# Other SBUF addresses: the values ahead of P, the turned inputs swapped, the pools of mixer and spatial stage in another sequence with empty stretches

## The chip, the cores and the metric

The kernel runs on one core of one Trainium2 chip. The metric is the device time of one execution in microseconds (us); three runs of the kernel before gave 2320.51, 2326.43 and 2330.06 us, so its median is 2326.43 us. Engines are named as in the profile: PE (TensorE matmul), PEld (its weight load), DVE (VectorE), ACT (ScalarE), POOL (GpSimd) and SP (SyncE, which here only issues DMAs, one after the other, in a fixed order).

## The reference, cut to what matters

Two different layers are applied in turn, twice over, to an input x of 2048 rows of 640 numbers:

```
x = x + A(layernorm(x))     # attention, 32 heads of 20, four segments of 512 rows, with a memory
x = x + B(layernorm(x))     # gated MLP with a mixing over the rows
x = x + A(layernorm(x))
x = x + B(layernorm(x))

A:  q, k, v = x @ wq, x @ wk, x @ wv
    for each segment: p = softmax(q k^T * scale + mask);  o = g * memory part + (1 - g) * p v
    return o @ wo
B:  z = gelu(x @ w_in);  z1, z2 = halves of z (864 wide each);  z2 = layernorm(z2)
    g = w_sp @ z2 + b_sp            # w_sp is 2048 x 2048: mixes the rows
    return (z1 * g) @ w_out
```

## The kernel before, in words

Each layer pair runs as three stages, one after the other in the program text. Large products are made from f16 parts: a number is split into a high part and the rest (h and l), and three products h*h, h*l, l*h are summed.

- **Attention** (`phase1a`, class `Attention`). Tiles of 128 rows are normalised (`prep`, L643), split, turned by a DMA transpose into `xt0` or `xt1` (segments take turns), and `value` (L663) multiplies them into `vs0` or `vs1`, first tiles 0 to 3, then the rest while the loop runs. `unit` makes q and k; the loop makes logits twice, exponentials into `P` and `Pb` (L909), their split into PH (L943) and PL (L945), the product with the values (L973). The o tiles go to DRAM (L1005). The projection with wo (`project`, L705) of tiles 0 to 11 fills PE; its rows stand in two buffers `xt` of pool `ae2` and are stored as x1 (L713).
- **Mixer** (`phase1b`). For each of 16 row tiles: layernorm, split (L264, L265), DMA transpose into `th` (L266), 30 matmuls with each half of w_in (L341), gelu, and the second half normalised and kept in SBUF as `zh` and `zl` (L349, L350), the first half stored to DRAM as z1 (L355). For tiles 12 to 15 the projection with wo is done here (L318), from tiles `o` and `xt`. In the first layer pair the first half of w_in is split here into `wi0h` and `wi0l` from five staged pieces `wst` (L115 load, L80 on ACT, L81 on DVE); in the second it is read back already split.
- **Spatial stage** (`phase2`). For each of 16 row tiles of w_sp, `rows(t)` loads 1 MB into `wr` (one buffer, L402), takes the row maxima on DVE (L404), scales and splits into `wn` (two buffers, L414 on ACT, L415 on DVE) and turns it by two DMA transposes into `wt` (two buffers, L416). `spatial(t)` does 96 matmuls `gp` (L427) over all of zh and zl, adds the bias (L430), multiplies with `cz1`, the reloaded z1 (L432), takes maxima (L434), splits (`un`, L440, L441) and turns (`ut`, L443). `tail(t)` does 42 matmuls `cyp` with w_out (L456), adds `cx1`, the reloaded x1 (L459), and stores the result. `spatial(t)` stands in the program ahead of `rows(t + 1)`, that ahead of `tail(t - 1)`.

**What sets the order.** In attention PE's order is written out by hand. Everything else (DVE, ACT, POOL, SP always, PE in the other stages) is ordered when the kernel is built: a planner plays the program through with its own durations, and each engine's next instruction is the ready one of highest priority, where earlier in the program is higher and `high_priority(offset=n)` counts as n instructions earlier. `rows(0)` and the loading of wi0 have the offset 2000, the first steps of the mixer 300; the mixer's whole program is about 1800 instructions long. On the chip each engine then works through its list strictly in that order, and waits at the first instruction whose inputs are not there.

**What addresses have to do with it.** SBUF is a stack: pools of a stage lie one behind the other in the sequence in which they are opened, pools with `side="right"` from the other end. When a stage ends its pools go, and the next stage's pools lie on the same bytes. With `reuse_waits="tile"` a new tile waits for exactly those earlier tiles whose bytes it covers. So a tile's address decides which last uses of the stage before it waits for. These are the places in bytes of a partition, summed from the sizes of the tiles (each rounded up to 32):

```
attention, before                      attention, after
 44064 qk0-4, vs1, mxs                  44064 the same
 65312 P                                65312 vs0
 85792 PL, rs, ab                       75808 PL, rs, ab
 93600 PH, gm                           83616 PH, gm
108960 mr                               98976 mr
109472 vs0                              99488 P
119968 phq, hl, tmp, den, mst, pk      119968 the same
145312 ae2: xt, xh (two each)          145312 xt1
155552 xt0                             155552 xt0
165792 xt1                             165792 ae2: xt, xh (two each)
176032 staging, qk5, Pb                176032 the same, to 193536

mixer, before (zh 44064, zl 71712)     mixer, after (zh, zl the same)
 99360 z1 z1, z2                        99360 z1 z1, z2
109728 x1 x1                           109728 o
114848 th th th                        112288 empty, 7808 bytes
122528 xn, xnhl                        120096 x1 x1
127648 wi0h, wi0l                      125216 th th th
144928 wst wst                         132896 xn, xnhl
151840 xt xt                           138016 wst wst
156960 o, to 159520                    144928 wi0h, wi0l
                                       162208 xt xt, to 167328

spatial stage, before                  spatial stage, after
 99360 u, un, ut                        99360 the same
109984 cz1 cz1, cx1 cx1, xo xo         109984 the same
127136 wuh, wul, bsp                   127136 the same
145120 wr                              145120 empty, 22336 bytes
153312 wn wn                           167456 wr
161504 wt wt, to 177888                175648 wn wn
                                       183840 wt wt, to 200224
```

From the right end, unchanged: `wi1h`, `wi1l` at 212064, `woh`, `wol` at 199264, both until the mixer ends, and in the spatial stage the staging of w_out at 222432.

Of the kernel before, what the change touches and what calls it, by code (L numbers as in the profile page):

```python
# [8 lines left out]
F32 = mybir.dt.float32  # L9
# [272 lines left out]
def phase1b(g, o_d, x, x1_d, z1_d, zh, zl):  # L282
    nc, tc = g.nc, g.tc
    with ExitStack() as ctx:
        pool = lambda n, b, **k: ctx.enter_context(tc.tile_pool(name=n, bufs=b, reuse_waits="tile", **k))
        p2, p1, pe2, pe3, pe1 = pool("b2", 2), pool("b1", 1), pool("be2", 2), pool("be3", 3), pool("be1", 1)
        wp0, sp, px2, px1 = pool("bw0", 1), pool("bs", 2), pool("bx2", 2), pool("bx1", 1)
        pz1, py, pz0 = pool("bz1", 2, space=PSUM), pool("by", 1, space=PSUM), pool("bz0", 1, space=PSUM)
        g.wi[0].tiles(wp0)
        wi0 = g.wi[0].load(sp)  # L290
# [87 lines left out]
def phase2(g, w_sp, b_sp, x1_d, z1_d, zh, zl, out):  # L378
    nc, tc = g.nc, g.tc
    KO = 7  # L380
    with ExitStack() as ctx:
        pool = lambda n, b, **k: ctx.enter_context(tc.tile_pool(name=n, bufs=b, reuse_waits="tile", **k))
        p1, p2, wp = pool("c1", 1), pool("c2", 2), pool("cw", 1)
        pr, ph, pt2, sp = pool("cr", 1), pool("ch", 2), pool("ctr", 2), pool("cs", 2, side="right")
        pg = pool("cg", 2, space=PSUM)
        py = pool("cy", 2, space=PSUM)
# [184 lines left out]
class Attention:  # L571
# [40 lines left out]
    def setup(self, ctx):  # L612
        g, nc, tc = self.g, self.nc, self.tc
        pool = lambda n, b, **k: ctx.enter_context(tc.tile_pool(name=n, bufs=b, reuse_waits="tile", **k))
        sk, p3, self.pl2, self.pl3, self.pr = pool("ak", 1), pool("a3", 1), pool("al2", 2), pool("al3", 3), pool("amr", 1)
        av, self.u4, self.u2, self.u1 = pool("av", 1), pool("au4", 4), pool("au2", 2), pool("au1", 1)
        self.e2, self.e1, ax = pool("ae2", 2), pool("ae1", 1), [pool(f"ax{i}", 1) for i in range(2)]
        self.pl1, self.bg = pool("al1", 1), pool("abg", 2)
        self.pd = pool("apd", 2, space=PSUM)
        self.px = pool("apx", 1, space=PSUM)  # L620
        self.pm = pool("apm", 1, space=PSUM)
        self.pe = pool("ape", 1, space=PSUM)
        self.po = pool("apo", 1, space=PSUM)
        more = pool("aqk", 1)
        self.Pb = pool("aP", 1).tile([128, 2, 1280], F32, name="Pb")
        self.qk = [(sk if i < 5 else more).tile([128, 2, L], F16, name=f"qk{i}") for i in range(self.NQK)]
        self.Pf = p3.tile([128, 2, 2, 1280], F32, name="P")
        self.vs = [p.tile([128, 4, H, 2 * DH + 1], F16, name=f"vs{i}") for i, p in enumerate((av, sk))]
        for t in self.vs:
            nc.gpsimd.memset(t[:, :, :, DH:DH + 1], 1.0)  # L630
        self.xt = [p.tile([128, 2, KD, L], F16, name=f"xt{i}") for i, p in enumerate(ax)]
        self.mxs = [sk.tile([128, 64], F32, name=f"mxs{i}") for i in range(2)]
        self.mst = [self.u1.tile([128, NU, 8, DH + 1], F32, name=f"mst{i}") for i in range(2)]
# [602 lines left out]
```

## Time and profile before

| | |
|---|---|
| median of three runs | 2326.43 us |
| the profiled execution: its own time | 2327.81 us |
| the profiled execution: span from first to last instruction | 2326.0 us |
| PE busy | 2171.9 us (93%) |
| DVE, ACT, POOL busy | 1375.1, 1139.1, 987.1 us |

The page of the profile gives busy times, the span in 40 slices and the costliest groups; the chain of waits is followed back from the last instruction to what released each step. A timeline lists instructions in order with their start and length, and in square brackets how long the engine had been idle and what ended that. A table by windows gives for each stretch its bounds, its length, each engine's busy time with its number of instructions, the granted TensorE clock, and the DMA engines' share and rate. All times in these views count from the start of the span.

### The profile page before, as it was taken

What the parts mean: (1) busy time and instruction counts of PE and PEld (TensorE: products, weight loads), DVE (VectorE), ACT (ScalarE), POOL (GpSimd) and SP (SyncE); (2) the same over time, 40 slices, a digit from 0 to 9 for tenths busy, and PEclk for the clock granted to TensorE, in tenths of its full rate; (3) what the DMA queues carried; (4) which work ended last, traced back from release to release, by engine and by line L of the source; (5) the groups of instructions that cost most, each with busy time, mean ns of one, the idle gap of its engine ahead of it and who ended that gap; (6) DMA issues with size and microseconds to landing.
All of it is one profiled execution on the core that took longest, in us unless ns stands there. A gap on an engine that the chain in (4) does not pass through costs nothing.

```text
span 2326.0 us, 52573 instructions
## 1 busy us (share of the span) xinstructions
PE 2171.9 (93%) x21706; PEld 1306.4 (56%) x21706; DVE 1375.1 (59%) x2577; ACT 1139.1 (49%) x1344; POOL 987.1 (42%) x976
## 2 busy tenths in 40 slices
PE   5888899999899999999998989999999999999998
PEld 3455555666555545555554556566665554555554
DVE  7688879677544545443427786877765453544331
ACT  3587788887522322121126987888863221112110
POOL 2387889999511000000014988899991100000000
PEclk9999999999999999999999999999999999999999
DMA  5565665345644587665534465443564347666561
GB/s 168 153 159 149 165 176 130 88 124 145 167 109 100 145 232 170 164 166 150 134 90 114 110 161 128 124 106 109 134 163 108 94 116 216 163 164 159 156 148 44
DMA packets 504912, 325.59 MB, mean 140 GB/s; under 512 B 410688, under 2 KB 445632, under 8 KB 499552
## 3 DMA queue, kind: packets, MB, share of 16 engines
q1 hardware_dynamic: 504672, 322.23, 53.9%
q8 instruction: 170, 2.79, 0.5%
q14 instruction: 70, 0.57, 0.1%
HBM read 148.46 MB, written 85.61 MB: 101 GB/s over the span
## 4 chain that ended last, share of the span: by engine, by line
PE 61%; DVE 12%; DMA 9%; POOL 7%; ACT 6%; issue 4%; SPq 2%; DVEq 0%; ACTq 0%; POOLq 0%
PE gp L427 19%; PE zp L341 13%; PE cyp L456 7%; POOL PL L945 5%; PE qps L732 3%; PE pv L973 3%; DMA wr<-in_B_w_sp_dram 3%; PE vps L673 2%; PE kps L732 2%; PE mp L871 2%; DVE mxs L934 2%; PE yps L705 2%; ACT P L909 2%; ACT PH L943 2%; PE es L871 1%
## 5 line engine op out<-in xcount | busy, mean ns | idle before, releaser
L945 POOL TENSOR_TENSOR PL<-P,PH 128x640 f16<-128x640 f32 x380 | 536.2, 1436 | 53.1 <-PE pv L973 43.6
L427 PE MATMUL gp<-zh,wt 128*128 128x432 f16 x2048 | 463.3, 346 | 4.5 <-DMA wt<-wn 4.5
L427 PEld LDWEIGHTS <-wt 128*128 128x128 f16 x3072 | 300.4, 98 | 262.6 <-DMA wt<-wn 5.3
L934 DVE TENSOR_REDUCE mxs<-mp 128x2 f32<-128x1024 f32 (+2 forms) x384 | 320.3, 862 | 136.4 <-PE mp L862 134.9
L909 ACT ACTIVATE P<-es,sc 128x1024 f32<-128x1024 f32 (+1 forms) x256 | 271.6, 1061 | 95.4 <-PE es L862 87.4
L442 POOL MEMSET un<- 128x64 f16 x32 | 5.0, 155 | 692.6 <-DMA ut<-un 648.0
L341 PEld LDWEIGHTS <-th 128*128 128x128 f16 x1920 | 187.5, 98 | 166.4 <-issue 3.5
L427 PE MATMUL gp<-zl,wt 128*128 128x432 f16 x1024 | 270.6, 346 | 0.0
L943 ACT CAST PH<-P 128x1280 f16<-128x1280 f32 x192 | 239.7, 1248 | 1.6
L252 POOL TENSOR_TENSOR lnrs<-lnve,mhalf 128x1 f32<-128x1 f32 x96 | 59.8, 631 | 423.8 <-DVE lnve L251 410.2
L430 ACT ACTIVATE u<-gp,bsp,un 128x864 f32<-128x864 f32 x32 | 34.2, 1068 | 363.3 <-PE gp L427 360.4
L404 DVE TENSOR_REDUCE am<-wr 128x1 f32<-128x2048 f32 x32 | 73.1, 2286 | 221.9 <-DMA wr<-in_B_w_sp_dram 221.9
L456 PE MATMUL cyp<-wuh,ut 128*128 128x320 f16 (+1 forms) x896 | 170.1, 308 | 14.1 <-DMA ut<-un 14.0
L945 POOL TENSOR_TENSOR PL<-Pb,PH 128x640 f16<-128x640 f32 x124 | 178.6, 1467 | 8.1 <-PE pv L973 8.0
L673 PE MATMUL vps<-wvh,xt 128*128 128x320 f16 x640 | 156.9, 314 | 26.7 <-DVE relu L764 19.2
L456 PEld LDWEIGHTS <-ut 128*128 128x128 f16 (+1 forms) x1344 | 134.6, 101 | 75.3 <-DMA ut<-un 16.8
L414 ACT ACTIVATE wn<-wr,ivw 128x1024 f16<-128x1024 f32 x64 | 72.0, 1144 | 204.5 <-DVE ivw L409 129.6
L871 PEld LDWEIGHTS <-qk 64*128 64x128 f16 (+1 forms) x2048 | 78.5, 94 | 159.5 <-issue 140.1
L973 PE MATMUL pv<-vs,PL 128*128 128x41 f16 x2560 | 157.0, 181 | 7.5 <-POOL PL L945 5.2
L973 PE MATMUL pv<-vs,PH 128*128 128x41 f16 x2560 | 159.4, 182 | 2.8 <-DVE ab L989 2.8
L341 PE MATMUL zp<-wi0h,th 128*128 128x432 f16 x640 | 148.5, 346 | 1.1 <-ACT z L354 1.1
L341 PE MATMUL zp<-wi1h,th 128*128 128x432 f16 x640 | 148.0, 346 | 1.3 <-DMA th<-xnhl 1.3
(189 smaller groups left out, 4347.4 us busy)
## 6 DMA issues: line engine op xcount, KB each, us to landing
wr<-in_B_w_sp_dram SPq DMA_DIRECT2D x32, 1024.0 KB
qk<-st SPq DMA_DIRECT2D x256, 120.0 KB
z<-z SPq DMA_DIRECT2D x32, 432.0 KB
cz<-z SPq DMA_DIRECT2D x32, 432.0 KB
xt<-in_A_x_dram SPq DMA_DIRECT2D x32, 320.0 KB
st<-qhl SPq DMA_DIRECT2D x40, 256.0 KB
st<-khl SPq DMA_DIRECT2D x40, 256.0 KB
x<-x SPq DMA_DIRECT2D x32, 320.0 KB
```

Source lines behind the costliest of these rows:

```text
L341: nc.tensor.matmul(zp[:, n, :FHH], a[:, k, :], b[:, k, c:c + FHH], start=(k == 0 and j == 0), stop=(k == KD - 1 and j == 2))
L404: nc.vector.tensor_reduce(am, wr, AX.X, ALU.max, apply_absolute_value=True)
L427: nc.tensor.matmul(gp[:, n, :FHH], wt[:, k // 8, a, k % 8, :], b[:, k, n * FHH:(n + 1) * FHH], start=(k == 0 and j == 0), stop=(k == NT - ...
L456: nc.tensor.matmul(yp[:, n, :320], a[:kn[k], k, :], b[:kn[k], k, n * 320:(n + 1) * 320], start=(k == 0 and j == 0), stop=(k == KO - 1 and ...
L673: nc.tensor.matmul(ps, a[:, k, c], b[:, k, n * 320:(n + 1) * 320], start=(i == 0), stop=(i == 14))
L732: nc.tensor.matmul(ps, a[:, k, c], b[:, k, :], start=(i == 0), stop=(i == 14))
L871: nc.tensor.matmul(out[:, h, o:o + w], a[r, ac], b[r, bc], start=o == 0, stop=False, skip_group_check=True)
L909: self.lead.append(nc.scalar.activation(P, E, AF.Exp, scale=g.esc))
L934: e = nc.vector.tensor_reduce(mx[:, :, n, j], mp[:, :, o:o + w], AX.X, ALU.max)
L943: nc.scalar.copy(PH, P[:, h])
L945: (nc.gpsimd if h == 0 or n < self.N - self.TAIL else nc.vector).tensor_tensor(PL[:, c], P[:, h, c], PH[:, c], ALU.subtract)
L973: nc.tensor.matmul(pv[:, i, h, :], x[:, c:c + 128], v[:, j, h0 + h, :], start=(j == 0 and x is PH), stop=(j == i and x is PL), skip_group_ ...
```

## The change

Only pools and their sequence change; every instruction's operation and shape stays. In attention the pool of `vs0` moves ahead of the pool of `P`, `xt1` comes ahead of `xt0`, both ahead of `ae2`, and the pool `ae1`, which held nothing, is gone. In the mixer `o` moves to the front, an empty stretch follows, the staging comes ahead of wi0, and `xt` goes last. In the spatial stage an empty stretch goes in ahead of `wr`. The tiles named gap are never written or read.

```
 phase1b
-        p2, p1, pe2, pe3, pe1 = pool("b2", 2), pool("b1", 1), pool("be2", 2), pool("be3", 3), pool("be1", 1)
-        wp0, sp, px2, px1 = pool("bw0", 1), pool("bs", 2), pool("bx2", 2), pool("bx1", 1)
+        p2, p1, px1, gap = pool("b2", 2), pool("b1", 1), pool("bx1", 1), pool("bgap", 1)
+        pe2, pe3, pe1 = pool("be2", 2), pool("be3", 3), pool("be1", 1)
+        sp, wp0, px2 = pool("bs", 2), pool("bw0", 1), pool("bx2", 2)
+        gap.tile([128, 1945], F32, tag="gap", name="gap")
 phase2
-        p1, p2, wp = pool("c1", 1), pool("c2", 2), pool("cw", 1)
+        p1, p2, wp, gap = pool("c1", 1), pool("c2", 2), pool("cw", 1), pool("cgap", 1)
+        gap.tile([128, 5580], F32, tag="gap", name="gap")
 Attention.setup
-        sk, p3, self.pl2, self.pl3, self.pr = pool("ak", 1), pool("a3", 1), pool("al2", 2), pool("al3", 3), pool("amr", 1)
-        av, self.u4, self.u2, self.u1 = pool("av", 1), pool("au4", 4), pool("au2", 2), pool("au1", 1)
-        self.e2, self.e1, ax = pool("ae2", 2), pool("ae1", 1), [pool(f"ax{i}", 1) for i in range(2)]
+        sk, av, self.pl2, self.pl3, self.pr, p3 = pool("ak", 1), pool("av", 1), pool("al2", 2), pool("al3", 3), pool("amr", 1), pool("a3", 1)
+        self.u4, self.u2, self.u1 = pool("au4", 4), pool("au2", 2), pool("au1", 1)
+        ax1, ax0, self.e2 = pool("ax1", 1), pool("ax0", 1), pool("ae2", 2)
+        ax = ax0, ax1
```

## The prediction

> **What bounds the kernel now.** I read the page first, then PE's idle time by windows, then the chain of waits, and last the timeline at each gap. From the page, the span and PE:
>
> ```profile
> span 2326.0 us, 52573 instructions
> PE 2171.9 (93%) x21706; PEld 1306.4 (56%) x21706; DVE 1375.1 (59%) x2577; ACT 1139.1 (49%) x1344; POOL 987.1 (42%) x976
> ```
>
> PE is busy 93%. An edit that only moves addresses changes no instruction, so it can win only where PE waits for something that an address decides, and an address decides only what a stage's first tiles wait for. So I cut the span at the joints of the stages. Columns: stretch, its length, then busy time of PE, PEld, DVE, ACT, POOL with counts, granted clock, DMA share and rate.
>
> ```profile
> 618.00:809.00 191.00, 186.70 (x1052) 102.57 (x1051) 101.13 (x197) 60.21 (x69) 19.73 (x30) 1.00 0.48 130
> 809.00:860.00 51.00, 45.52 (x242) 24.56 (x241) 23.88 (x40) 14.29 (x16) 0.30 (x2) 0.90 0.84 228
> 860.00:1173.00 313.00, 313.00 (x1857) 181.34 (x1855) 131.73 (x234) 54.45 (x52) 7.13 (x20) 1.00 0.64 157
> 1173.00:1206.00 33.00, 29.64 (x205) 20.41 (x204) 11.58 (x26) 7.09 (x12) 6.92 (x7) 0.95 0.40 97
> 1750.00:1936.00 186.00, 186.00 (x1052) 102.72 (x1051) 96.31 (x192) 56.79 (x65) 18.81 (x30) 1.00 0.43 109
> 1936.00:2060.00 124.00, 116.69 (x662) 65.65 (x661) 52.90 (x93) 23.64 (x23) 0.91 (x6) 0.97 0.77 198
> ```
>
> Inside the mixer and the spatial stage PE never rests (313.00 of 313.00, 186.00 of 186.00). It rests at three joints: start of the spatial stage in the first pair (809 to 860) and in the second (1936 to 2060), and the passage from the first spatial stage to the second attention (1173 to 1206). There the clock is below 1 as well. The gaps one by one, from PE's timeline:
>
> ```profile
> 841.15 0.90 PE L427 MATMUL gp<-zh,wt 128*128 128x432 f16 x2 [2.11 <-DMA wt<-wn]
> 845.42 0.71 PE L456 MATMUL cyp<-wuh,ut 128*128 128x320 f16 x2 [3.37 <-DMA ut<-un]
> 1184.05 0.45 PE L456 MATMUL cyp<-wuh,ut 128*128 128x320 f16 x2 [0.93 <-DMA ut<-un]
> 1192.36 0.30 PE L673 MATMUL vps<-wvh,xt 128*128 128x320 f16 x1 [2.43 <-DVE vs L679]
> 1968.58 0.54 PE L427 MATMUL gp<-zh,wt 128*128 128x432 f16 x2 [2.38 <-DMA wt<-wn]
> 1973.08 0.45 PE L456 MATMUL cyp<-wuh,ut 128*128 128x320 f16 x2 [2.32 <-DMA ut<-un]
> 2045.40 0.45 PE L456 MATMUL cyp<-wuh,ut 128*128 128x320 f16 x2 [2.51 <-DMA ut<-un]
> ```
>
> After such a gap the next matmuls run slowly: windows over L456 alone (length, PE busy, PEld busy, clock, DMA) show the same 42 matmuls in 8.79, 7.56 and 7.55 us at clock 0.68 and 0.79, and in 5.88 us at clock 1.00.
>
> ```profile
> 845.00:855.00 10.00, 8.79 (x42) 5.21 (x42) 0.68 0.72 232
> 1973.00:1981.00 8.00, 7.56 (x42) 4.71 (x42) 0.79 0.44 174
> 2045.00:2053.00 8.00, 7.55 (x42) 4.73 (x42) 0.79 0.86 174
> 1184.00:1190.00 6.00, 5.88 (x42) 4.03 (x42) 1.00 0.41 128
> ```
>
> The Trainium skill, "TensorE: Matmul & The Clock Gate", Part 1, puts the drop to half clock after an idle window of about 3.4 us; taken as a threshold, only the gap of 3.37 us could carry a tail. The trace disagrees: gaps of 2.32 to 2.51 us carry one too. By the threshold the sum below would lose its tails after those gaps, 3.35 + 1.41 us; by the rows they stand, and I take the rows.
>
> **Start of the spatial stage.** The chain of waits shows what is late there (start, length, what), and a full mixer tile and a full gp for measure:
>
> ```profile
> 746.57 10.95 PE zp L341 x60
> 817.10 9.79 DMA wr<-in_B_w_sp_dram
> 877.07 17.52 PE gp L427 x96
> 1922.31 6.18 DMA wr<-in_B_w_sp_dram
> 1945.31 12.13 DMA wr<-in_B_w_sp_dram
> ```
>
> The third w_sp tile, for gp(2), is requested at 817.10 and 1945.31, when the stage has begun. On DVE, the reduce that waits for it stands ahead of the steps for u(0):
>
> ```profile
> 826.91 2.29 DVE L404 TENSOR_REDUCE am<-wr 128x1 f32<-128x2048 f32 x1 [2.29 <-DMA wr<-in_B_w_sp_dram]
> 829.89 1.06 DVE L432 TENSOR_TENSOR u<-u,cz 128x864 f32<-128x864 f32 x1
> 1953.93 1.06 DVE L432 TENSOR_TENSOR u<-u,cz 128x864 f32<-128x864 f32 x1 [17.83 <-DMA cz<-z]
> 833.96 6.82 SPq L416 DMA_TRANSPOSE wt<-wn  x2
> 840.88 2.10 SPq L443 DMA_TRANSPOSE ut<-un  x1
> ```
>
> So wt(2) is turned from 833.96, after PE has almost finished gp(1), and ut(0) only behind it at 840.88; PE waits for both. In the second pair the first wait on DVE is for cz1. Addresses cause this. Before, `wr` at 145120 and `wn` at 153312 cover the mixer's `wst`, `xt` and `o`, and `xt` and `o` serve tiles 12 to 15, the mixer's end. So rows(0) can't begin before that, and as wr is one buffer, rows(1) and rows(2) follow one load each later. After, wr, wn and wt begin at 167456, behind the mixer's last byte (167328). Only attention's tiles lie there, gone since the mixer began; wt's second buffer also touches woh, whose last use is tile 15's projection in the mixer. So rows(0), rows(1) up to its transposes, and wr(2) have the whole mixer for themselves, and wt(2) waits for gp(0) alone. The `cz1` and `cx1` tiles before cover x1 and th of the mixer; after, mostly `o` and the empty stretch, so their loads too can go ahead of the crowd.
>
> If so, both waits go in both pairs. First pair: 2.11 + 3.37 = 5.48 us idle plus 8.79 - 5.88 = 2.91 us of slow pace: 8.4. Second pair: 2.38 + 2.32 + 2.51 = 7.21 idle plus (7.56 - 5.88) + (7.55 - 5.88) = 3.35: 10.6. Together 19.0. What is late next is the ut chain of some later tile, which has one whole gp (17.5 us) of cover; I take nine tenths, **17 us**.
>
> **Spatial stage to second attention.** Before, `vs0` at 109472 covers ut, both cz1 and both cx1; all are in use until the last tail. So the values of tile 0 stand in PSUM until L459 is done:
>
> ```profile
> 1190.32 0.88 DVE L459 SCALAR_TENSOR_TENSOR xo<-cyp,xs,cx 128x640 f32<-128x640 f32 x1
> 1191.24 0.78 ACT L678 ACTIVATE vs<-vps 128x320 f16<-128x320 f32 x2
> ```
>
> ACT starts 0.04 us after it. After, vs0 at 65312 covers zh and zl, free when gp(15) ends, and its memset on POOL (L630) comes forward with it. Then value tile 1 follows tile 0 (the 30 matmuls in the first row below), fills the wait for ut of 0.93 us, and the 2.43 us go. For tiles 2 and 3 to be in time, xt0 must be filled earlier: before it covers wn and wt; after, the empty stretch, so its transposes wait for nothing. The pace:
>
> ```profile
> 1178.00:1184.00 6.00, 4.24 (x30) 2.93 (x30) 1.00 1.12 230
> 1192.00:1199.00 7.00, 6.64 (x37) 4.33 (x38) 0.76 0.54 143
> ```
>
> 37 of these at the first row's pace take 5.23 us, so 1.41 are lost. Sum 0.93 + 2.43 + 1.41 = **4.8 us**.
>
> **Attention to mixer, first pair.** `wst` before covers `pk` and the `xt` and `xh` buffers of ae2, which the last projection and the last o tile use; its loads go out behind that store, and PE waits for the split once:
>
> ```profile
> 612.45 0.95 SPq L115 DMA_DIRECT2D wst<-in_B_w_in_dram  x2
> PE zp L341 <- DVE wi0l L81: 1.9, 1, 1.9
> ```
>
> After, wst covers mst and pk, whose last reads come with the last segment's memory, steps ahead of attention's end. **1.9 us** gained. But the five splits, by their priority, now run inside attention:
>
> ```profile
> L81 DVE SCALAR_TENSOR_TENSOR wi0l<-wst,iv,wi0h x5: 1108/1112/1118, 619.6 to 633.3; 128x864 f16<-128x864 f32 x5
> L81 DVE SCALAR_TENSOR_TENSOR wol<-wst,iv,woh x5: 876/1179/1706, 250.8 to 265.9; 128x640 f16<-128x640 f32 x5
> ```
>
> The same operation takes up to 1706 ns inside attention and 876 at best. The Trainium skill, "SBUF — State Buffer", Who interferes with whom, has a rule against this move: a DVE instruction with two SBUF inputs and a GpSimd one that reads SBUF block each other for the whole instruction. The slowest wol row agrees. By the rule at its worst all five take what that row shows, and the gain would be smaller by 10.8 - 1.9 = 8.9 us. My cost goes by rows: between 0 (hidden, as PE is the busier engine) and 5 x 1.112 x 1706/876 = 10.8 us (all on the path). The nearest row is wol's median, 1179 against 876, a third more: 5 x 1.112 x 0.35 = **1.9 us**, which I take.
>
> **What the early rows cost.** They come at the mixer's start, where before they ran at its end, hidden. Of rows(t) DVE does:
>
> ```profile
> L404 DVE TENSOR_REDUCE am<-wr x32: 2279/2286/2289, 781.8 to 2227.5; 128x1 f32<-128x2048 f32 x32
> L415 DVE SCALAR_TENSOR_TENSOR wn<-wr,ivw,wn x64: 1273/1280/1286, 787.0 to 2241.8; 128x1024 f16<-128x1024 f32 x64
> DVE am L404 <- DMA wr<-in_B_w_sp_dram: 221.9, 31, 11.3
> ```
>
> That is 2.29 + 2 x 1.28 = 4.9 us, and ahead of the reduce DVE stood still 221.9/31 = 7.2 us on average: the planner lists it before the load has landed. What is queued behind it on DVE is the layernorm and split of the next th tile, and PE waits for that. At most 12.1 us per row; a mixer tile takes 10.95 us of PE and 53% of DVE (101.13 of 191), so 5.1 us of DVE are free per tile and at most 7.0 come through. At least 0, as in the second pair before, where the load of 1922.31 and the one ahead of it were taken in between 1750 and 1936 and PE lost nothing. ACT has 60.21 us of work in 191, so its two scalings per row hide. Rows(0) has priority over the whole mixer and meets it where th is not yet ahead; I take **2 us** in each pair, and nothing for rows(1) and rows(2), which come last in priority. SP's list gains nothing, its DMAs only move; it passes th's transposes, in the same 2 us. The mixer's other moves (x1, th, xn over phq, hl, tmp; zl over PL, PH, gm; z2 over P) cover tiles done before the first write; they cost nothing. If gm's last use were late, zl would wait, and PE not, as zl is needed only by gp. In the first attention the moves wait for nothing, as no stage came ahead.
>
> **Sum.** 17 + 4.8 + 1.9 - 1.9 - 4 = 17.8 us. The profiled execution took 2327.81 us, 1.4 above the median of 2326.43; on the median's basis 2326.43 - 17.8 = **2308.6 us**. Bounds of the terms: with all of 19.0 and no cost 25.7, so 2301; with costs of 10.8 and 2 x 7.0 the 23.7 are eaten and 1.1 more, so 2328.
>
> **Rivals.**
> - *The gain is given back at the mixer's start.* Rows(0) costs its full 7.0 us in both pairs and the splits half of their upper bound, 5: 23.7 - 14 - 5 = 5 us gained, 2322. For it: the 7.2 us that DVE stood before L404. Against: the full stretch of 1750 to 1936, above, with two such loads in it. Chance 0.17.
> - *The planner does not use the freedom.* It still lists the loads late, or wn and wt bind; then the passage to the second attention remains and, say, three tenths of the start: 4.8 + 0.3 x 19 - 2 = 8 us, 2318. For it: rows(1) and rows(2) come last in priority. Against: the load at 1922.31 is rows(1)'s and was issued inside the mixer, ahead of the stage's start at 1936. Chance 0.14.
> - *Slower.* Rows(0), (1) and (2) each hold DVE inside the mixer beyond its 5.1 us of slack per tile and PE waits each time: 3 x 7.0 x 2 = 42, less 23.7, 18 us more, 2345. It decides once the standstill per row passes about 5 us inside the mixer. Against: DMA there is busy 0.43 to 0.48, at the spatial start 0.84, so loads should land sooner than the 7.2. Chance 0.09.
>
> My forecast has the remaining 0.60, with 2297 to 2317 as its own range.
>
> **How the numbers follow.** Half a per cent of the median, 11.6 us, is about what a measurement of this kernel can tell from no change: faster means below 2314.8, slower above 2338.1. Faster: 0.55 of the forecast's 0.60, 0.07 of the second rival, 0.02 of the first: 0.64. Slower: 0.09. Same: 0.27. The range runs from 2294 (planner luck in attention beyond the bounds) to 2326, which takes in the first two rivals and leaves out the slower one and the tails, under 0.2.
>
> **What would show it.** In the changed profile: three wr loads ahead of 809 and of 1936, the first soon after attention's end; no PE gap ended by wt or ut in the spatial stage's first 60 us of either pair; vs0's ACT right after its matmuls, and value tiles in one run at clock 1; L115 for wi0 well ahead of 612. Wrong would be: new PE gaps ended by th between 615 and 660 or 1745 and 1790, with DVE standing before L404; a longer first attention; or gaps at the spatial stage's start that stay.

## The result, and the profile after

The changed kernel takes 2315.67 us (median of nine runs, 2304.89 to 2320.03) where the kernel before takes 2327.17 (nine runs beside it, 2320.51 to 2333.34). The recorded ratio is 0.9936, 95% interval 0.9923 to 0.9949: 15 us or 0.64% faster (0.0064 x 2327), 12 to 18 by the interval; the two medians by themselves are 11.5 us apart. Its profiled execution is the slowest of the nine, 2320.03 us, so a second profile was taken (run e8 below, 2311.18 us). Three executions far off all others (5012.18 us of run e10, which was the profiled one, and 2770.27 and 12151.94 us of the kernel before, beside later runs) are left out of the ratios.

The page of the changed kernel, span and engines:

```profile
span 2318.3 us, 52548 instructions
PE 2174.6 (94%) x21706; PEld 1309.5 (56%) x21706; DVE 1377.8 (59%) x2577; ACT 1139.2 (49%) x1344; POOL 991.4 (43%) x976
```

The five engines' counts are those of before; the 25 fewer of the total are instructions that do not count as busy. The table by windows, over the same stretches of work as before, shifted to where they now lie:

```profile
624.50:812.00 187.50, 185.15 (x1045) 101.90 (x1044) 100.33 (x200) 58.03 (x66) 18.38 (x28) 1.00 0.52 127
812.00:863.00 51.00, 50.15 (x287) 27.77 (x285) 25.40 (x41) 14.85 (x16) 0.30 (x2) 1.00 0.87 237
1164.00:1197.00 33.00, 33.00 (x234) 22.77 (x233) 9.01 (x17) 5.25 (x9) 1.39 (x3) 1.00 0.22 55
1753.00:1941.00 188.00, 183.53 (x1036) 100.83 (x1034) 101.12 (x200) 57.35 (x65) 18.37 (x28) 1.00 0.48 117
1941.00:2065.00 124.00, 124.00 (x727) 70.99 (x726) 50.27 (x89) 22.88 (x22) 0.91 (x6) 1.00 0.72 177
```

All three joints are closed. At the spatial starts PE is busy 50.15 of 51 us (before 45.52) and 124.00 of 124 (before 116.69), in the passage 33.00 of 33 (before 29.64), and the granted clock is 1.00 where it was 0.90, 0.95 and 0.97. In return the second mixer, full before (186.00 of 186.00), now has 4.47 us in which PE stands idle. The gaps that are left, from PE's timeline:

```profile
594.86 0.61 PE L875 MATMUL es<-qk 64*128 64x384 f16 x4 [2.59 <-ACT P L913]
645.73 0.54 PE L343 MATMUL zp<-wi1h,th 128*128 128x432 f16 x2 [1.29 <-DMA th<-xnhl]
791.40 0.54 PE L343 MATMUL zp<-wi1h,th 128*128 128x432 f16 x2 [1.06 <-DMA th<-xnhl]
847.54 0.44 PE L459 MATMUL cyp<-wuh,ut 128*128 128x320 f16 x2 [0.85 <-DMA ut<-un]
1759.58 0.54 PE L343 MATMUL zp<-wi1h,th 128*128 128x432 f16 x2 [0.89 <-DMA th<-xnhl]
1773.14 0.54 PE L343 MATMUL zp<-wi1h,th 128*128 128x432 f16 x2 [2.43 <-DMA th<-xnhl]
1918.90 0.54 PE L343 MATMUL zp<-wi1h,th 128*128 128x432 f16 x2 [1.15 <-DMA th<-xnhl]
```

(`zp` is the mixer's product with w_in. Line numbers are those of each kernel's own file; the changed kernel's lie 2 to 4 above those of before.) Of the seven gaps at the joints one of 0.85 us is left. The longest inside attention's end is now 2.59 us, and five gaps in the mixers are ended by th; the second mixer had none before.

The clearest account is the length of each stage from PE's own records: the mixer M from its first zp to its last; S from there to the last gp; the passage P from there to the last matmul of value tile 3 of the next attention; A from the span's start, or from the passage's end, to the first zp. The last column ends with the last cyp. Times in us of one profiled execution each:

| kernel | A1 | M1 | S1 | P | A2 | M2 | S2, tail included |
|---|---|---|---|---|---|---|---|
| before | 607.4 | 201.2 | 364.8 | 33.1 | 533.1 | 196.2 | 386.3 |
| changed | 613.6 | 199.5 | 356.2 | 27.7 | 541.9 | 201.8 | 373.7 |
| changed, second profile (e8) | 613.0 | 199.2 | 356.3 | 27.7 | 536.0 | 200.4 | 372.9 |
| e1 spatial stage alone | 606.4 | 202.1 | 362.8 | 30.9 | 533.2 | 198.7 | 374.2 |
| e2 attention alone | 621.5 | 198.3 | 363.9 | 39.8 | 541.4 | 198.3 | 383.7 |
| e3 mixer alone | 605.4 | 197.6 | 382.8 | 32.7 | 533.3 | 197.0 | 400.8 |
| e7 changed, attention put back | 605.3 | 206.7 | 363.9 | 30.9 | 537.6 | 206.3 | 373.2 |
| e4 changed, wi0 later | 601.4 | 206.1 | 356.6 | 27.7 | 535.7 | 200.1 | 373.9 |
| e5 changed, rows(0) at tile 8 | 612.1 | 199.8 | 356.0 | 27.7 | 533.6 | 198.1 | 373.8 |
| e6 changed, rows(0) at tile 3 | 613.6 | 197.8 | 356.2 | 27.7 | 537.9 | 198.2 | 374.1 |
| e9 as e6, wt clear of woh | 615.3 | 202.2 | 356.6 | 27.7 | 537.1 | 202.3 | 374.6 |
| e12 as e9, rows apart | 617.4 | 200.1 | 356.4 | 27.7 | 533.4 | 198.6 | 374.5 |
| e11 as e1, x of attention later | 612.7 | 202.3 | 356.4 | 32.6 | 533.5 | 198.7 | 373.8 |

S and P repeat within 0.8 us between the two profiles of the changed kernel, M within 1.4; A does not: old and unchanged attention pools alone gave 605 to 613 for A1 and 533 to 538 for A2. So the stages other than attention are read from profiles, and totals from the timed ratios.

How much a wait at the mixer's start costs can't be read at its third tile, because PE fills part of such waits with matmuls of the projection with wo (`yp`) that it would else do later: 30 of them in the first three tiles of the first mixer before, 24 in both mixers of the changed kernel, 14 where nothing waits; 30 take 4.1 us. By the start of tile 12 all kernels have done the same work. Counted from the mixer's first zp to there, in us:

| kernel | first mixer | second mixer |
|---|---|---|
| before | 144.51 | 139.55 |
| changed | 141.01 | 143.22 |
| changed, second profile (e8) | 140.70 | 141.85 |
| e1 | 143.76 | 140.17 |
| e4 | 147.69 | 141.55 |
| e5 | 141.25 | 139.55 |
| e6 | 139.55 | 139.55 |

139.55 us is thus a mixer without waits up to there. In the rest of the mixer, the changed kernel loses 1.3 us in each pair to a gap near the end, and does three gp more (0.5 us) before the last zp; those are taken from S.

### The profile page after: what moved, and what is told of

It is laid out like the page before. It is cut to its first block, busy times and chain, and to the rows that moved or that the text cites. A ratio compares the mean times of both kernels' runs of the same rounds, so it can differ in the third digit from the quotient of the medians.

```text
span 2318.3 us, 52548 instructions
## 1 busy us (share of the span) xinstructions
PE 2174.6 (94%) x21706; PEld 1309.5 (56%) x21706; DVE 1377.8 (59%) x2577; ACT 1139.2 (49%) x1344; POOL 991.4 (43%) x976
## 3 DMA queue, kind: packets, MB, share of 16 engines
q8 instruction: 170, 2.79, 0.5%
## 4 chain that ended last, share of the span: by engine, by line
PE 66%; DVE 9%; DMA 8%; POOL 6%; ACT 6%; issue 3%; SPq 1%; DVEq 0%; ACTq 0%; POOLq 0%
PE gp L430 23%; PE zp L343 13%; PE cyp L459 8%; POOL PL L949 5%; PE pv L977 3%; PE qps L736 3%; PE kps L736 3%; PE vps L677 3%; PE mp L875 3%; DVE mxs L938 2%; PE yps L709 2%; PE es L875 2%; ACT P L913 1%; ACT PH L947 1%; DMA th<-xnhl 1%
## 5 line engine op out<-in xcount | busy, mean ns | idle before, releaser
L949 POOL TENSOR_TENSOR PL<-P,PH 128x640 f16<-128x640 f32 x380 | 538.8, 1444 | 53.2 <-PE pv L977 45.6
L949 POOL TENSOR_TENSOR PL<-Pb,PH 128x640 f16<-128x640 f32 x124 | 178.0, 1462 | 9.2 <-PE pv L977 9.2
L459 PE MATMUL cyp<-wuh,ut 128*128 128x320 f16 (+1 forms) x896 | 165.1, 301 | 5.7 <-DMA ut<-un 5.7
L459 PEld LDWEIGHTS <-ut 128*128 128x128 f16 (+1 forms) x1344 | 132.1, 98 | 61.5 <-DMA ut<-un 6.4
L875 PE MATMUL es<-qk 64*128 64x512 f16 (+3 forms) x1024 | 126.3, 303 | 31.7 <-ACT P L913 27.1
```

Source lines behind the costliest of these rows:

```text
L459: nc.tensor.matmul(yp[:, n, :320], a[:kn[k], k, :], b[:kn[k], k, n * 320:(n + 1) * 320], start=(k == 0 and j == 0), stop=(k == KO - 1 and ...
L875: nc.tensor.matmul(out[:, h, o:o + w], a[r, ac], b[r, bc], start=o == 0, stop=False, skip_group_check=True)
L949: (nc.gpsimd if h == 0 or n < self.N - self.TAIL else nc.vector).tensor_tensor(PL[:, c], P[:, h, c], PH[:, c], ALU.subtract)
```

## The experiments

**Three parts, one at a time (e1, e2, e3).** Of e1 the edit is

```
+        gap.tile([128, 5580], F32, tag="gap", name="gap")    # spatial stage only
```

and e2 and e3 are the kernel before with attention's or the mixer's lines of the diff alone.

> The kernel before, with one line of the change: the empty stretch ahead of wr in the spatial stage; the mixer's and attention's pools stay. Theory (wr's address alone decides the start of the spatial stage, and it also brings the cost at the mixer's start): the spatial start is 8 us shorter in the first pair and 11 in the second, as in the changed kernel; the two waits for wr and th at the mixer's start come with it, about 1 to 5 us in each pair; the passage to the second attention and the end of the first attention stay as before. Together about 12 us below the kernel before. Rival (the moves of cz1, cx1 and the mixer's o are needed too): less than half of that, under 6 us, with gaps left at the spatial start.

e1 took 2320.49 us, ratio 0.9968 (0.9954 to 0.9982): 7.5 us, about two thirds of what the theory gave. Both spatial starts closed as in the changed kernel (up to the 480th gp the first gained 7.6 us, the second 11.4 by its end), so wr's address alone does that; the rival falls. The cost at the mixer's start, expected at 1 to 5 us per pair, is 0.6 in the second pair by tile 12 and none in the first. But S1 as a whole gained 2.0 only. SP's timeline of e1 shows why:

```profile
859.83 0.32 SPq L649 DMA_DIRECT2D xt<-x  x1
1005.68 0.32 SPq L649 DMA_DIRECT2D xt<-x  x1
```

From 859.83 to 1005.68 seven x tiles for the second attention are loaded, normalised and turned, on DVE and SP, between the spatial stage's own steps, and PE waits (3.34 us for ut at 936.21 alone). In e1 attention's `ae2` still lies at 145312, on the new empty stretch, and may be filled at any time. The changed kernel's `ae2` lies on `wr`, so its first such load comes at 1128.46.

> The kernel with the spatial stage's empty stretch alone, and one more edit: the loads of x for the second attention are planned behind the store of tile 12's result. Theory (with the old attention pools ae2 lies on the empty stretch, so seven x tiles were normalised and turned between 860 and 1010, ahead of the spatial stage's own steps on DVE and SP; PE waited 3.3 us at 944 and the stage lost 6.2 us; in the changed kernel ae2 lies on wr's bytes and waits by itself): the loss of 6.2 us between gp 480 and the last gp of the first pair goes to under 1, the rest stays; 4 to 7 us below the kernel with the empty stretch alone. Rival (that loss has another cause, such as cz and cx at their old places): it stays.

> The kernel with the spatial stage's empty stretch alone and x's loads for the second attention planned behind the store of tile 12's result, once more, since the first profile of it fell on an execution of 5012 us. Theory: between gp 480 and the last gp of the first pair nothing is lost against the kernel before (6.2 us were, without the second edit), both spatial starts keep their gain, and the time is 4 to 7 us below that of the empty stretch alone. Rival: the loss stays.

The edit, on top of e1:

```
             s = nc.sync.dma_start(out[t], xo.rearrange("p n c -> p (n c)"))
+            if t == 12:
+                g.late = s
 # in prep, from the second attention on
+            c2.enter_context(self.tc.issue_after(g.late.ins))
             nc.sync.dma_start(xt, self.x[t])
```

e10 took 2316.69 us (median of all five), ratio 0.9940 (0.9916 to 0.9963). e11, the same kernel, took 2310.65 us, ratio 0.9927 (0.9907 to 0.9946): 6.5 and 9.6 us below e1, each against the kernel before (0.0028 and 0.0041 of 2330). In e11's profile the loads come at 1137.29 and later and S1 is 356.4, with nothing lost after the 480th gp. So the loss was the early x tiles. This kernel keeps the old attention and mixer and is about as fast as the whole change.

> The kernel before, with the attention pools of the change alone. Theory (vs0 clear of cz1 and cx1 is what makes the passage shorter): the passage from the first spatial stage to the second attention is 4 to 5.4 us shorter, all gaps at both spatial starts stay as before. wst at 144928 then covers pk and xt1, so the wi0 splits may come forward too; if they do, the first attention ends some 5 us later and the first mixer's start is some 4 us shorter, near zero together. In all 4 to 6 us below the kernel before. Rival (the passage is shorter in the changed kernel because the spatial stage's own tail moved): no change at the passage, 0 in all.

e2 took 2352.24 us, ratio 1.0107 (1.0082 to 1.0131): 25 us slower, both theory and rival wrong. PE's timeline:

```profile
621.52 0.90 PE L341 MATMUL zp<-wi1h,th 128*128 128x432 f16 x2 [7.66 <-DMA th<-xnhl]
1197.70 0.71 PE L456 MATMUL cyp<-wuh,ut 128*128 128x320 f16 x2 [8.25 <-DMA ut<-un]
```

and SP's:

```profile
606.78 0.80 SPq L300 DMA_DIRECT2D x<-x  x2
1170.23 13.87 SPq L649 DMA_DIRECT2D xt<-x  x2
```

P at 99488 to 119968 now lies under the old mixer's z1 and x1, and P is read until attention's last steps: x for the mixer's first tile is loaded at 606.78 and PE stands 7.66 us, in the second pair 6.1. In the passage SP stands 13.87 us in front of a load of x for attention, and the last `ut`, next in SP's list, is late by 8.25: attention's new `ae2` (165792) lies on the old `wt` (161504 to 177888), which the last gp reads until 1183.75. So the mixer's `o` and its empty stretch (109728 to 120096) do no work of their own: by the addresses they keep x1 and th off P, which attention's move has put there.

> The kernel before, with the mixer pools of the change alone. wr at 145120 then lies on wi0h and wi0l (144928 to 162208), which are read until the last mixer tile. Theory (an address decides when a stage's first load may begin): rows(0) cannot start before the mixer's last matmuls, so gp(0) waits for a load of 1 MB, the reduce, the scalings and two transposes, about 15 to 20 us in each pair: 30 to 40 us slower than the kernel before. Rival (loads come when the planner lists them, addresses matter little): within 5 us of the kernel before.

e3 took 2358.73 us, ratio 1.0139 (1.0113 to 1.0164): 32 us slower, as the theory said. PE's timeline:

```profile
818.51 0.90 PE L429 MATMUL gp<-zh,wt 128*128 128x432 f16 x2 [15.47 <-DMA wt<-wn]
1968.56 0.90 PE L429 MATMUL gp<-zh,wt 128*128 128x432 f16 x2 [19.78 <-DMA wt<-wn]
```

With wr under wi0, rows(0) can't start before the mixer's last matmuls, and PE stands 15.47 and 19.78 us. This is the address mechanism by itself, with the sign turned round.

**All but attention (e7).** The changed kernel with attention's old lines.

> The changed kernel with attention's pools put back: mixer and spatial stage as changed. Theory (each part's terms add up): both spatial starts keep 8 and 11 us, the passage to the second attention loses its 5.4, the first attention's end and the first mixer's start go back to before (+4.8 and -4.3 both gone), the rows at the mixer's start cost some us per pair; 4 to 8 us slower than the changed kernel, 7 to 12 below the kernel before. Rival (parts depend on each other: with the old attention, wr at 167456 lies on xt1 and xt0 on the empty stretch, so other work comes forward): the sum fails by more than 5 us in some stage that the theory leaves unchanged.

e7 took 2329.57 us, ratio 1.0014 (0.9999 to 1.0030): nothing is left of the gain. The rival holds. S1 has the early x tiles of e1, and both mixers are longer than in any other kernel, 206.7 and 206.3. e7's chain of waits, second pair:

```profile
1750.76 5.05 DMA o<-ohl
1755.83 5.17 DMA wi0l<-w_i0l
```

wi0 at 144928 lies on the old ae2, whose last reader is the end of attention; wi0l is read back only behind the last o store, from 1755.83, when the mixer's first zp (1744.3) is 11.5 us past. With the new attention that place is xt1's and xt0's. Parts that are worth -0.32% (e1), +1.07% (e2) and +1.39% (e3) alone make -0.64% together: an address is right only beside its neighbour's.

**The attention's end (e4).** The first attention's end loses 4.8 us (between the seventh and the last eighth of pv) in both profiles of the changed kernel, 4.8 to 6.3 in e2, e5, e6, e9 and e12, and 1.0 or less in e1, e3, e7 and e11, which have the old attention pools. DVE's splits there, grouped by form, in the changed kernel:

```profile
L81 DVE SCALAR_TENSOR_TENSOR wi0l<-wst,iv,wi0h x5: 1328/1458/2178, 578.3 to 594.0; 128x864 f16<-128x864 f32 x5
```

```
-            for _ in range(g.wi[0].nk + 1):
-                next(wi0, None)
+            with tc.issue_after(g.stored.ins):      # the last o store
+                for _ in range(g.wi[0].nk + 1):
+                    next(wi0, None)
```

> The changed kernel, with the loads of wi0's five pieces issued behind the last o store, as the trace of the kernel before shows them. Theory (the 4.8 us that the first attention's end lost are the five wi0 splits on DVE and ACT in the attention's tail, and the 4.3 us that the first mixer's start won are the same splits gone from there): the attention's end comes back by 4 to 5 us, the first mixer's start loses 4 us or some more, as rows(0) now meets the splits there; within 3 us of the changed kernel in all. Rival (the tail is slower because of the new addresses of P, xt1 and ae2): the attention's end stays 4.8 us late and the mixer's start loses as well, about 4 us slower than the changed kernel.

e4 took 2313.53 us, ratio 0.9945 (0.9924 to 0.9965). The attention's end takes 0.2 us less than in the kernel before, so the 4.8 are the splits; M1 grew from 199.5 to 206.1. By tile 12 it is 6.7 longer than in the changed kernel (147.69 against 141.01), where the splits cost 5.0 in the kernel before (144.51 against 139.55): beside rows(0) they cost 1.7 more. DVE of e4:

```profile
615.62 2.28 DVE L408 TENSOR_REDUCE am<-wr 128x1 f32<-128x2048 f32 x1
628.91 1.11 DVE L81 SCALAR_TENSOR_TENSOR wi0l<-wst,iv,wi0h 128x864 f16<-128x864 f32 x1
```

The sum changes little; the rival falls. The splits take 1.11 us here, and 1.33 to 2.18 in attention.

**The rows at the mixer's start (e5, e6).** e5 holds the load of rows(0) until the z1 store of tile 8; e6 is the same with `t == 3`.

```
+            s = nc.sync.dma_start(z1_d[t], z1)
+            if t == 8:
+                g.mid = s
-        with tc.high_priority(offset=HP):
+        with tc.high_priority(offset=HP), tc.issue_after(g.mid.ins):
             wt = rows(0)
```

> The changed kernel, with one edit: the first load of rows(0) in each pair is planned behind the store of z1 of mixer tile 8, so that it runs in the middle of the mixer and not at its start. Theory (what the mixer's start loses is DVE waiting for wr with the next th queued behind it): the waits of 0.89 and 2.43 us at the second mixer's start and their counterparts in the first go, and the whole gain at the spatial start stays, since eight tiles of 11 us remain for three rows: 5 to 7 us below the changed kernel. Rival (the mixer's start is slow for another reason, such as the splits of wi0 or the clock): the mixer's start stays as it is and the time is the changed kernel's.

> The changed kernel, with the first load of rows(0) in each pair planned behind the store of z1 of mixer tile 3 rather than tile 8 as in the run before it. Theory (rows(0) and rows(1) cost only where DVE has no slack ahead of PE: at the mixer's start, where th is not yet ahead, and from tile 12 on, where the projection with wo adds DVE work; tiles 4 to 11 left DVE 4.46 us idle per tile in the trace): no PE gap ended by th at either mixer's start nor between tiles 4 and 11, mixer steps of the changed kernel (+5.0 in the second pair) go to 0, and the first pair's loss of 5.8 us in the mixer's second half that the tile-8 run showed goes to under 3; the spatial starts keep 8 and 11 us: 6 to 9 us below the changed kernel. Rival (any wait of DVE for a 1 MB load costs PE wherever it stands): 3 to 6 us move to tiles 4 to 7 and the time is that of the tile-8 run.

e5 took 2309.24 us, ratio 0.9926 (0.9897 to 0.9955), e6 2308.95, ratio 0.9920 (0.9902 to 0.9938). In both the mixers' starts lose nothing any more: in e6 the first mixer gains 5.0 us by tile 12 against the kernel before (the changed kernel 3.5), and the second loses 0.0 (the changed kernel 3.7, in its second profile 2.3). In e5 the first mixer lost 1.7 by there, with a gap of 1.53 at 748.75. (The 5.0 and 5.8 of the expectation count shifted `yp` too.) DVE's timeline of e6:

```profile
673.29 2.27 DVE L409 TENSOR_REDUCE am<-wr 128x1 f32<-128x2048 f32 x1
685.77 2.29 DVE L409 TENSOR_REDUCE am<-wr 128x1 f32<-128x2048 f32 x1 [0.79 <-DMA wr<-in_B_w_sp_dram]
1792.87 2.27 DVE L409 TENSOR_REDUCE am<-wr 128x1 f32<-128x2048 f32 x1
1805.03 2.29 DVE L409 TENSOR_REDUCE am<-wr 128x1 f32<-128x2048 f32 x1 [0.48 <-DMA wr<-in_B_w_sp_dram]
```

Two rows at tiles 3 to 5 cost PE no gap there; DVE stood 0.79 us at most. M1 and M2 are 197.8 and 198.2, 1.7 and 3.6 below the changed kernel (1.4 and 2.2 below its second profile). The two intervals of the ratio overlap the changed kernel's: shown in the mixers, not in the total, and less than the 6 to 9 us that were expected.

**The row at the mixer's end (e9, e12).** e9 frees wt of woh; e12 holds four loads apart as well.

```
-        gap.tile([128, 5580], F32, tag="gap", name="gap")
+        gap.tile([128, 5324], F32, tag="gap", name="gap")
-                nc.sync.dma_start(wr, ...)
+                    c2.enter_context(tc.issue_after(g.z1s[(2, 5, 8, 15)[t]].ins))   # e12, t < 4
+                nc.sync.dma_start(wr, ...)
```

> The tile-3 run's kernel with two addresses moved: the mixer's xt pair goes into its empty stretch, and the spatial stage's empty stretch is 1024 bytes shorter, so that wt ends at 199200, below woh (199264). Theory (in the changed kernel the transposes of rows(0) wait for tile 15's projection, the last reader of woh, so wn is full until then and rows(2) is loaded only at the mixer's very end, where DVE stood 4.9 to 5.2 us for it and PE lost a gap of 0.9 to 1.2 with what follows): three rows are now loaded and scaled between tiles 3 and 7, where DVE has slack, the gap at the mixer's end goes, the mixer stage is 196 to 197 us long in each pair (tile-3 run 197.8 and 198.2, changed kernel 199.5 and 201.8); both spatial starts stay; 2 to 4 us below the tile-3 run, about 2305 to 2307 where the kernel before has 2328. Rival (the gap at the mixer's end has another cause, such as the last z1 and th transposes): the mixer lengths stay within 1 us and the time is the tile-3 run's.

> The kernel of the run before with wt clear of woh, and the four loads of wr planned apart: rows(0) behind the z1 store of mixer tile 2, rows(1) behind tile 5, rows(2) behind tile 8, rows(3) behind tile 15. Theory (in the packed run, four rows stood 1.5 tiles apart; each takes 4.9 us of DVE work and 0.7 to 2.7 us of waiting for its load, where a tile leaves DVE 4.46 us, so DVE fell behind and PE waited three times in the first pair and twice in the second; three tiles apart the slack of a tile or two pays for each row): no PE gap ended by th in tiles 3 to 11, mixer lengths 196 to 198 us where the packed run had 202.2 and 202.3; both spatial starts as in the changed kernel; 8 to 10 us below the packed run, about 2305 to 2309. Rival (the transposes of wt, 4 to 5 us each on SP ahead of th's, are what PE waits for): gaps stay at each row, one or two us each, and the mixers are 199 us or longer.

e9 took 2316.57 us, ratio 0.9945 (0.9926 to 0.9964), its mixers 202.2 and 202.3. The gap at the end did go, so it was wt's address on woh; but larger ones came. PE's timeline of e9:

```profile
691.46 0.54 PE L343 MATMUL zp<-wi1h,th 128*128 128x432 f16 x2 [0.73 <-DMA th<-xnhl]
715.16 0.54 PE L343 MATMUL zp<-wi1h,th 128*128 128x432 f16 x2 [1.61 <-DMA th<-xnhl]
730.03 0.54 PE L343 MATMUL zp<-wi1h,th 128*128 128x432 f16 x2 [3.07 <-DMA th<-xnhl]
```

e12 took 2313.26 us, ratio 0.9930 (0.9912 to 0.9947), its mixers 200.1 and 198.6: better than packed, not as good as e6, and not the 196 to 198 expected. One gap per pair is left, 2.06 us at 716.74 and 2.23 at 1834.62. SP's timeline of e12 ahead of the first:

```profile
707.83 5.34 SPq L424 DMA_TRANSPOSE wt<-wn  x2
713.27 1.35 SPq L266 DMA_TRANSPOSE th<-xnhl  x1
```

xnhl is written by 710.70 (DVE, 709.88 and 0.82 long), but SP stands in the two transposes of wt until 713.17; th comes 2.6 us late and PE waits 2.06. So the rival holds in part: wt's transposes on SP cost what DVE's wait had. Rows spread over the mixer are paid by whichever of DVE, SP or the transfers has no slack; how to get all three rows in for nothing stays open.

**The same kernel once more (e8).**

> The changed kernel once more, for a second profile. Theory (the 7.8 us that its first profile lost inside the second attention between 1206 and 1510 come from that one execution, since the order of the instructions there is the same as before and the granted clock was 0.95 and 0.97 against 1.00): the second profile has those stretches within 2 us of the kernel before, and its cyp ends 10 us or more below the kernel before's. Rival (the new addresses slow that attention): the 7 to 8 us are there again.

e8 took 2314.09 us, ratio 0.9942 (0.9924 to 0.9959). A2 is 536.0, not 541.9: of the 8.8 us that the first profile lost there, 5.9 belong to that execution. 2.9 remain, more than the 2 expected; but the other kernels with the same attention lines lie 0.3 (e12) to 4.8 (e6) above the kernel before, leaving out e2 with its wait at the mixer, and e7, with the old lines, 4.5.

## Where the prediction was right, and where its steps failed

The time, 2315.67 us, lies within the stated 2294 to 2326, 7 above the 2308.6. The predicted gain was 17.8 us; the timed ratios give 15 and 13.5 (0.0058 x 2328), the medians 11.5 and 13.8, both profiles 7.8 (2320.03 against 2327.81) and 16.6 (2311.18). Term by term:

- *Start of the spatial stage, 17.* Right, and too cautious: from the first gp on, the first start gained 8.1 us, the second 11.4, together 19.5, all of the 19.0 that the gaps and their slow tails added up to, so the taken nine tenths were not needed. e1 shows that wr's address does it and e3 that the wrong one costs 15 to 20. The three loads ahead of the first stage's start, as named, in SP's timeline of the changed kernel:

```profile
620.41 0.35 SPq L405 DMA_DIRECT2D wr<-in_B_w_sp_dram  x1
636.04 0.33 SPq L405 DMA_DIRECT2D wr<-in_B_w_sp_dram  x1
790.97 1.35 SPq L405 DMA_DIRECT2D wr<-in_B_w_sp_dram  x1
```

- *Passage, 4.8.* Right: 5.4 in both profiles (33.1 to 27.7), with ACT taking the values 2.0 us apart, as PE makes them, where it had waited for L459:

```profile
1177.05 0.45 ACT L682 ACTIVATE vs<-vps 128x320 f16<-128x320 f32 x1 [2.63 <-PE vps L677]
1179.08 0.45 ACT L682 ACTIVATE vs<-vps 128x320 f16<-128x320 f32 x1 [1.59 <-PE vps L677]
```

  Neither half of its reason was run by itself: the empty stretch under the old attention's xt0 gave 2.2 (e1; 0.5 in e11), and all of attention's moves without the spatial stage's, vs0's among them, made the passage 6.7 longer (e2), as ae2 then lay on wt. Only the parts together gave the 5.4.
- *wi0 at the first mixer, 1.9.* Right in kind, mis-sized: with the rows out of the way (e6) it is 5.0, as the splits had held back th and the gelu too: the kernel before has gaps of 1.90, 0.37, 1.07 and 0.96 us between 620 and 644, of which the prediction counted the first. L115 comes at 573.35, before at 612.45.
- *wi0's splits in attention, 1.9.* Mis-sized: 4.8. It lies inside the bounds of 0 and 10.8. The third that was added to each split is about right (five at a median of 1458 where 1112 ns were taken, 1.7 us); the rest is what stands behind them. For PE's 2.59 us at 594.86, which end with ACT's P, ACT had first stood 1.11 us for the last piece wst and then split it, 1.02 us at 591.63.
- *The early rows, 2 per pair.* The size is near, the account of it is not. By tile 12 the starts cost 1.5 us in the first pair (5.0 less 3.5) and 3.7 in the second (second profile 1.2 and 2.3), where 4 in all were taken. But rows(0), for which they were taken, is only the gap of 0.89 in the second pair. The failed step is "nothing for rows(1) and rows(2), which come last in priority": the gaps of 1.29 and 2.43 come with rows(1), and 1.3 us more are lost in each pair at the mixer's end. The changed kernel's DVE lists both rows at the start:

```profile
625.37 2.29 DVE L407 TENSOR_REDUCE am<-wr 128x1 f32<-128x2048 f32 x1 [0.77 <-DMA wr<-in_B_w_sp_dram]
643.07 2.29 DVE L407 TENSOR_REDUCE am<-wr 128x1 f32<-128x2048 f32 x1 [5.35 <-DMA wr<-in_B_w_sp_dram]
1752.14 2.29 DVE L407 TENSOR_REDUCE am<-wr 128x1 f32<-128x2048 f32 x1 [2.33 <-DMA wr<-in_B_w_sp_dram]
1770.53 2.29 DVE L407 TENSOR_REDUCE am<-wr 128x1 f32<-128x2048 f32 x1 [6.04 <-DMA wr<-in_B_w_sp_dram]
```

and its chain of waits shows that PE's two gaps there have two causes:

```profile
637.78 7.90 DMA th<-xnhl
1746.80 5.31 DMA wr<-in_B_w_sp_dram
1756.15 3.39 DMA th<-xnhl
1764.56 8.54 DMA th<-xnhl
```

  rows(0) makes DVE stand, as the prediction had it, and 0.89 us come through. rows(1)'s 6.04 us of standing cost nothing by themselves: th was issued before them, at 1764.56, but 1.75 us behind the 1 MB load of 1762.81, and took 8.54 us to land where the one before took 3.39. The same stands in the first pair at 637.78 (7.90 us, behind the load of 636.04). That gap, the larger (2.43), is a transfer behind a transfer, which the prediction did not count.

  At the mixer's end it is SP. The prediction had rows(0) turned early, with only rows(1)'s transposes held by woh. In the trace rows(0)'s own transposes come at 776.74 (in e9, with wt clear of woh, at 681.00), rows(1) is scaled and turned behind them, and the last th is between its two:

```profile
785.30 1.87 SPq L419 DMA_TRANSPOSE wt<-wn  x1
787.25 1.84 SPq L266 DMA_TRANSPOSE th<-xnhl  x1
```

  Its input xnhl was written by 785.97; th lands 4.10 us after its issue, and PE's gap of 1.06 ends at 791.40.
- *The second attention, nothing.* 2.9 us were lost in the second profile, 8.8 in the first; how much of that the addresses cause is not shown (e8 above, and below).

The errors ran both ways: 2.5 + 0.6 + 3.1 us more were gained than taken, and 2.9 + 1.1 + 2.6 + 2.9 more lost, which makes 14.5 of the 17.8. That the sum stood is in part luck. Of the signs of being wrong that it named, two came: gaps ended by th in both stretches, and a first attention that is longer (4.8 us at its end). Of the gaps at the spatial start one of 0.85 stayed.

Of the rivals, the one that gives the gain back at the mixer's start named a real cost: 1.5 + 3.7 + 4.8 = 10.0 us were paid there, but 29.9 came in (19.5, 5.4 and 5.0) where it counted 23.7. "The planner does not use the freedom" is refuted by the three loads, and the slower case by its own price: the rows at the starts cost 5.1 us where it counted 42. With e9 it has a grain of truth, as four rows packed behind each other cost some 4 us per mixer (202.2 and 202.3 against 197.8 and 198.2).

The rule cited from the Trainium skill, "TensorE: Matmul & The Clock Gate", Part 1, would have lost 3.35 + 1.41 us of the gain; the clock column at 1.00 and the full 19.5 show that the tails after the gaps of 2.3 to 2.5 us did go with them. "SBUF — State Buffer", Who interferes with whom, told rightly that the splits would be slower there. All five ran beside tensor operations of POOL that read SBUF (L949, L996, L997); but only one reached the 2.17 us that the prediction worked out as the worst (1.112 x 1706/876), the others took 1.33 to 1.53, and away from attention, in e4, 1.06 to 1.12.

## What to carry to other kernels

Where a tile's address makes it wait, list both sides: whom it waits for now, and what will come forward when it no longer waits; e1 lost 6 of its 8 us in one stage to work that had been held back by nothing but its address, and one explicit hold on top of it (e11) made it about as good as the whole rearrangement. Early loads should be placed where their consumer's engine, its queue and the transfers around it have slack, not as early as they can be; here that was tile 3, not tile 0, by 1.7 and 3.6 us of the mixers' lengths. Change addresses of neighbouring stages together and measure them together: two of the three parts by themselves made the kernel slower. And when comparing stages, mark them where the same work has been done, as PE may have moved work into a wait.

## What the runs showed of the hardware that was not expected

A DMA transpose of th issued 1.75 us after a 1 MB load took 8.54 us to land, one 1.74 us after another (637.78 behind 636.04) 7.90, and one 9 us after its load 3.39. Over the traces of the changed kernel, e5, e6, e8, e9 and e12, the fourteen that were issued within 1.8 us behind such a load took 4.40 to 8.54 us; those with none in the 15 us ahead have medians of 3.76 to 3.90. The distance alone does not set it: in e6 two at 1.74 and 1.76 us took 4.83 and 4.40. Nor must it be a load of 1 MB: before, one took 7.59 us, 1.66 behind the store of wi0l.

The first stretch of the second attention, from the passage's end to the first eighth of pv, took 106.1 to 106.2 us at a granted clock of 1.00 in all five kernels with the old attention pools (before, e1, e3, e7, e11), and 106.3 to 109.5 in the eight profiles with the new ones. Windows over it, kernel before:

```profile
1206.00:1313.00 107.00, 95.26 (x1227) 55.39 (x1225) 71.26 (x120) 71.63 (x93) 56.07 (x47) 1.00 0.42 110
```

the changed kernel, at a lower clock:

```profile
1197.00:1306.00 109.00, 97.89 (x1212) 56.20 (x1211) 70.50 (x118) 70.82 (x92) 55.31 (x46) 0.95 0.41 108
```

PE's work between those marks is the same, 1221 matmuls, which keep it busy 94.4 us before and 98.3 in the changed kernel; the clock is 0.95 to 0.98 in seven of the eight, and 1.00 in e12 (106.3 us). The lower mean is one piece of it at half clock, and it begins in a wait of PE for DVE or at most 1.4 us behind it. A window and PE's timeline of the changed kernel:

```profile
1215.00:1225.00 10.00, 8.42 (x48) 4.50 (x48) 3.03 (x5) 2.04 (x4) 1.40 (x1) 0.50 0.37 117
1216.05 0.43 PE L677 MATMUL vps<-wvh,xt 128*128 128x320 f16 x1 [3.20 <-DVE relu L768]
```

Every kernel has this wait. It is 2.77 to 2.79 us in the five with the old pools, and the clock stays at 1.00; 2.97 in e12, and it stays too; 2.76 to 3.44 in the seven where it drops. So a longer wait goes with the drop in most, but its length alone does not decide, as e9 drops with 2.76. Nor does the rest in the passage ahead: seven of the eight have none left there, e12 among them, and e2, with the longest passage, drops as well. Why the clock drops stays open; over this first eighth of pv the new pools gave back 0.2 to 3.4 of the 5.4 us that the passage had gained.
